# Stores on ScalarE's queue, softmax totals spread over groups, and a last product in two banks: one change to a fused attention and MoE kernel

## The chip, the cores and the metric

One Trainium2 chip, one core. The metric is the device time in microseconds of one execution; times are given as the median of several runs.

## The reference

Attention within chunks of 64 rows (no attention across chunks), the heads laid side by side as a row of 512, and a two-layer network with an exact GELU between:

```
q, k, v: (8, 8, 576, 64) float32          # batch, heads, rows, head size; 9 chunks of 64
attn = softmax(q_c @ k_c.T / sqrt(64))    # per chunk
x = (attn @ v_c) -> (4608, 512)
g = gelu_exact(x @ w_in)                  # w_in (512, 2048)
out = g @ w_out                           # w_out (2048, 512), out float32 (4608, 512)
```

## The kernel before

**Tiles.** The 4608 rows are worked in nine tiles of 512 rows, t = 0 to 8. Tile t < 8 holds chunks 0 to 7 of batch element t; tile 8 holds chunk 8 of all eight elements. Products run on TensorE in bf16.

**Order.** The kernel writes out the order of every engine's instructions by hand (a manual schedule): each engine runs its own instructions in the order in which the program emits them, and waits where data or a buffer is missing. For each tile, `phase` first runs mm1 (`x @ w_in`), sixteen groups f = 0 to 15 of four matmuls (L419), each followed by one GELU on ScalarE (L421), and then mm2 (`g @ w_out`). The attention of the next tile, n = t + 1, is hung into these as hooks: `extra1` (e1) maps a group f of mm1, and `extra2` (e2) a slot of mm2, to things to emit just before it.

**mm2.** For t = 1 and 2, mm2 is `mm2_slot`: four blocks of 128 rows, each in four slots (16 slots; L557), and `rows_out` evicts a block to `y_sb` and stores it. From t = 3, `mm2_seven` does the product with seven instead of eight block products (Strassen's scheme in Winograd's form): steps s = 0 to 6 of two slots each, so hooks stand at slots 0 to 13. The sums of blocks that it needs come from VectorE (`g_sum`, L461 and L474, and `weight_sum`). Banks "a", "b" and "d" hold products; "a" is written in steps 0, 2, 4 and 6, "b" in step 1, "d" in steps 3 and 5. `keep` copies a bank to SBUF (ScalarE, L491), `done` adds a kept block to a bank and stores it (VectorE, L495), `last` evicts the seventh (L500), and `last_piece` does so in halves in the last tile.

**Attention of tile n.** `quad_S` makes the scores in 64 small matmuls (L227), four exps on ScalarE (L234), and for each exp a 32x32 transpose and a sum on VectorE (`quad_part`, L249 and L252). `quad_total` brings the partial sums together: eight small copies on ScalarE (L262), a sum and a reciprocal on VectorE (L265, L267), and four copies on ScalarE (L272); `quad_rc` spreads the reciprocals (L276). `quad_av` multiplies by v (64 small matmuls, L283), and `quad_x` scales the result to x (VectorE, L290). Where `quad_S(n + 1)` follows `quad_av(n)` directly, the two are one joint burst of small matmuls.

**PSUM.** Eight banks in three pools: `ps_mm` (3), `ps_tp` (2), `ps_at` (3). `four_banks` takes two of `ps_at` and two of `ps_tp`; with `beside_av`, `quad_S` takes one of `ps_at` and three of `ps_mm`.

**Loads and stores.** All loads, all transposing DMAs (`flip`, L194) and nearly all stores are issued by SyncE (SP), in program order. Loads land as float32 in six staging buffers, GpSimd (POOL) casts them to bf16, and `flip` transposes q and k of a tile. q and k are brought three tiles ahead (`bring_qk(t + 3)`). `y_sb` and `kept` share four buffers. ScalarE loads another function table when it goes between exp and GELU (`act_table`, L653).

Of the kernel before, what the change touches and what calls it, by code (L numbers as in the profile page):

```python
# [11 lines left out]
def kernel(  # L12
# [9 lines left out]
    nc = tc.nc  # L22
    P = 128
# [5 lines left out]
    CH = 64  # L29
# [225 lines left out]
    def quad_total(t):  # L255
# [3 lines left out]
        for g2 in range(2):  # L259
            for s in range(G):  # L260
                o = s ^ 1
                nc.scalar.copy(part[g2][QD * s:QD * (s + 1), :, :, :, 1], part[g2][QD * o:QD * (o + 1), :, :, :, 0])  # L262
        for g2 in range(2):
# [3 lines left out]
            nc.vector.reciprocal(rb[:], total[:])  # L267
            tiles[t]["rb", g2] = rb[:, 0], across[g2][:]
            if g2 == 0:
                quad_rc(t, 0, 0)  # L270
            for r in range(2):
                nc.scalar.copy(across[g2][CH * r:CH * (r + 1)], rb[CH * (1 - r):CH * (2 - r), 1])  # L272
# [153 lines left out]

    HF = FF // 2
# [48 lines left out]
    def mm2_seven(t, hooks):  # L476
# [10 lines left out]
        bank, kept = {}, {}  # L487

        def keep(name, of):
            kept[name] = ypool.tile([P, HM, HD], f32, tag="y", name="kept")  # L490
            nc.scalar.copy(kept[name][:], bank[of][:])  # L491

        def done(r, c, of, plus):
            y_sb = ypool.tile([P, HM, HD], f32, tag="y", name="y_sb")
            nc.vector.tensor_tensor(y_sb[:], bank[of][:], kept[plus][:], op=ADD)  # L495
            store_block(t, r, c, y_sb)

        def last():
            y_sb = ypool.tile([P, HM, HD], f32, tag="y", name="y_sb")
            nc.scalar.copy(y_sb[:], bank["a"][:])  # L500
            store_block(t, 1, 0, y_sb)
# [8 lines left out]
        for s, (name, left, right, then) in enumerate(steps):  # L510
            fresh = name not in bank
            for m in range(HM):
                for u in hooks.get(HM * s + m, ()):
                    u()
                if fresh and m == 0:
                    pool, tag = (ps_mm, "mm") if name == "d" or t == NT - 1 else (ps_tp, "tp")
                    bank[name] = pool.tile([P, HM, HD], f32, tag=tag, name="y_ps")
                for f in range(HF):
                    nc.tensor.matmul(bank[name][:, m], left(f, m), right[:, f],  # L519
                                     start=(fresh and m == 0 and f == 0),  # L520
                                     stop=(f == HF - 1), skip_group_check=True)
                if t == NT - 1 and s == len(steps) - 1:
                    last_piece(t, m, bank["a"][:, m])
            if not (t == NT - 1 and s == len(steps) - 1):
                then()

    def store_block(t, r, c, y_sb):
        cols = slice(HD * c, HD * (c + 1))
        if t < B:
            m0 = t * S + HD * r  # L530
            nc.sync.dma_start(out[m0:m0 + HD, cols].rearrange("(m p) d -> p m d", p=P), y_sb[:])
            return
        for m in range(HM):
            for i in range(P // CH):
                m0 = ((HM * r + m) * (P // CH) + i) * S + MT
                nc.sync.dma_start(out[m0:m0 + CH, cols], y_sb[i * CH:(i + 1) * CH, m])

    def last_piece(t, m, y_ps):
        y_sb = ypool.tile([P, HD], f32, tag="y", name="y_sb")
        n = HD // 2  # L540
        if m == 0:
            nc.scalar.copy(y_sb[:], y_ps)
        else:
            nc.vector.tensor_copy(y_sb[:, 0:n], y_ps[:, 0:n])
            nc.scalar.copy(y_sb[:, n:HD], y_ps[:, n:HD])
        for i in range(P // CH):
            m0 = ((HM + m) * (P // CH) + i) * S + MT
            (nc.sync if i == 0 else nc.scalar).dma_start(out[m0:m0 + CH, 0:HD], y_sb[i * CH:(i + 1) * CH])
# [16 lines left out]
    def store(t, ms, y_sb):  # L565
        m0 = t * S + ms * P
        nc.sync.dma_start(out[m0:m0 + P, :], y_sb[:])

    def rows_out(t, ms):
        y_ps = tiles[t]["y_ps", ms]  # L570
        y_sb = ypool.tile([P, d_model], f32, tag="y", name="y_sb")
        (AC if ms < 3 else DV)(y_sb[:], y_ps[:])  # L572
        if t == 0 and ms == 2:
            act_table(Act.Gelu)
        if t == 0:
            held.append((ms, y_sb))
        else:
            store(t, ms, y_sb)
# [76 lines left out]
    with tc.manual_schedule():  # L655
# [108 lines left out]
        def last_av():  # L764
            A[3]()
            rows_out(0, 3)
            store(0, *held.pop())
# [11 lines left out]
        for t in range(1, NT):  # L779
# [3 lines left out]
            if t == 1:  # L783
# [3 lines left out]
                for ms, y_sb in held:  # L787
                    store(0, ms, y_sb)
                held.clear()
                load_v_rows(2, (1,))  # L790
            elif t == T0:
                flip_qk(t + 2)
            if n < NT:
                cast_v_rows(n, PO)
            if t == 1:
                bring_qk(t + 2)
                bring_qk(t + 3)
                flip_qk(t + 2)
            if t > 1 and t + 3 < NT:
                bring_qk(t + 3)  # L800
# [5 lines left out]
            flip_next = lambda: flip_qk(t + 3) if t + 3 < NT else None  # L806
            xs = [lambda m=m: quad_x(n, m // 2, m % 2) for m in (1, 3, 0, 2)]
            if t < T0:
                e1 = {f: [lambda i=i: weight_sum(i)] for i, f in ((1, 6), (2, 8), (3, 10), (4, 12))}
                e2 = {0: [exp, lambda: quad_S(n)], 3: [total], 5: [gelu],  # L810
# [3 lines left out]
            elif t == T0:  # L814
                e2 = {0: [exp, lambda: quad_S(n)], 3: [total],
                      8: [lambda m=m: quad_rc(n, m // 2, m % 2) for m in range(1, G)],
                      12: [av] + xs + [lambda: quad_S(n + 1, True)], 13: [flip_next], 15: [gelu]}
            else:
                g = [[lambda i=i, a=a: g_sum(t, i, a) for i in (1, 2, 4)] for a in range(2)]
                e1 = {9: [lambda: g_sum(t, 3)], 13: g[0]}  # L820
                e2 = {0: g[1][:2], 2: g[1][2:]}
                if n < NT:
                    if t == T0 + 1:
                        e1[3] = [total]
                    e1[5] = [lambda m=m: quad_rc(n, m // 2, m % 2) for m in range(1, G)]
# [41 lines left out]
```

## Time and profile before

| | |
|---|---|
| median of 3 runs | 284.04 us (283.96 to 285.39) |
| profiled execution | 286.06 us, its span 284.0 us |
| mean granted TensorE clock | 0.99 |
| TensorE matmuls busy | 270.3 us (95%) |
| ScalarE, VectorE, GpSimd busy | 180.7, 159.3, 91.7 us |
| DMA moved | 53.89 MB, 190 GB/s on the mean |

The profile names engines PE (TensorE matmuls), PEld (its weight loads), DVE (VectorE), ACT (ScalarE), POOL and SP; SPq and ACTq are the instruction queues that issue DMAs. Times are microseconds from the span's start. In a row in order of time stand start, length, engine, line, operation, output<-input, sizes and count, and in brackets the idle time before it and what ended it. A busy matmul is not one at its peak, since matmuls are pipelined and their ends are modelled. "Granted clock" is the share of TensorE's full speed that its throttle allowed.

### The profile page before, as it was taken

The page shows a single profiled execution, that of the slowest core. Times are in us where ns is not written, and L with a number is a line of the kernel's source. Part 1 is how long each engine was busy: PE and PEld are TensorE (multiplying, and loading weights), DVE is VectorE, ACT ScalarE, POOL GpSimd, SP SyncE. Part 2 cuts the span into 40 slices and gives each one's busy share as a digit, 9 for nine tenths or more (in the row PEclk, how much of TensorE's full clock was granted, in tenths as well). Part 3 has the DMA queues.
Part 4 walks back from the last instruction along what each step waited for, and adds up shares of the span by engine and source line. Part 5 has one row for each costly group of instructions (what it writes and reads, how often), then busy time and mean ns, then how long its engine had stood idle before and what let it go on. Part 6 is the DMA issues. An engine that isn't in the chain of part 4 may idle for free.

```text
span 284.0 us, 6437 instructions
## 1 busy us (share of the span) xinstructions
PE 270.3 (95%) x2589; PEld 160.7 (57%) x2589; DVE 159.3 (56%) x267; ACT 180.7 (64%) x370; POOL 91.7 (32%) x146
## 2 busy tenths in 40 slices
PE   6799999999999999799999999999999999999991
PEld 2464455444444444248844874587458745864781
DVE  5865358835900299448915992598159816311620
ACT  3766758877647667666676657757775766347410
POOL 6868778831542206304404610451011000000000
PEclk9999999999999999899999999999999999999998
DMA  7999998999789799999999998979430310130024
GB/s 222 253 360 402 393 362 234 226 254 239 179 235 244 238 262 240 241 212 255 220 285 237 168 204 177 176 168 260 107 84 2 113 35 2 39 111 0 2 46 102
DMA packets 122477, 53.89 MB, mean 190 GB/s; under 512 B 97872, under 2 KB 118352, under 8 KB 122448
## 3 DMA queue, kind: packets, MB, share of 16 engines
q1 hardware_dynamic: 122288, 53.36, 72.8%
q8 instruction: 20, 0.33, 0.5%
q10 hardware_dynamic: 160, 0.13, 0.2%
q14 instruction: 9, 0.07, 0.1%
HBM read 36.70 MB, written 9.44 MB: 162 GB/s over the span
## 4 chain that ended last, share of the span: by engine, by line
PE 87%; ACT 3%; DVE 2%; DMA 2%; POOL 2%; SPq 1%; issue 1%; DVEq 0%; ACTq 0%
PE h_ps L419 41%; PE y_ps L519 25%; PE y_ps L557 11%; PE y_ps L593 3%; PE h_ps L409 2%; DMA arrival<-in_k_dram 2%; POOL v_bd L169 2%; PE s_ps L227 1%; PE av_ps L283 1%; SPq L114 1%; PE tp L175 1%; ACT h L421 1%; DVE x L290 1%; PE av_ps L374 1%; ACT y_sb L572 1%
## 5 line engine op out<-in xcount | busy, mean ns | idle before, releaser
L419 PE MATMUL h_ps<-x,w_in_sb 128*128 128x512 bf16 x548 | 121.9, 383 | 2.2 <-ACT h L421 2.2
L421 ACT ACTIVATE h<-h_ps 128x512 bf16<-128x512 f32 x137 | 80.9, 598 | 38.0 <-PE h_ps L419 37.7
L419 PEld LDWEIGHTS <-w_in_sb 128*128 128x128 bf16 x548 | 54.0, 99 | 67.7 <-issue 5.0
L164 POOL CAST q_nat<-arrival 128x512 bf16<-128x512 f32 x31 | 19.9, 682 | 62.9 <-DMA arrival<-in_q_dram 41.9
L557 PE MATMUL y_ps<-w_out_sb,h 128*128 128x512 bf16 x144 | 32.4, 379 | 0.0
L519 PEld LDWEIGHTS <-h 128*128 128x128 bf16 x288 | 27.9, 98 | 5.1 <-issue 1.2
L200 POOL CAST v_nat<-arrival 128x1024 bf16<-128x1024 f32 x14 | 15.0, 1075 | 48.4 <-DMA arrival<-in_v_dram 30.2
L461 DVE TENSOR_TENSOR s_sb<-h 128x2048 bf16<-128x2048 bf16 x6 | 7.4, 1226 | 35.8 <-ACT h L421 35.8
L491 ACT COPY kept<-y_ps 128x512 f32<-128x512 f32 x18 | 10.6, 586 | 23.2 <-PE y_ps L519 22.0
L653 ACT ACT_TABLE_LOAD x18 | 23.1, 1283 | 1.1 <-PEq L851 0.7
L519 PE MATMUL y_ps<-w_out_sb,h 128*128 128x256 bf16 x192 | 22.0, 272 | 0.7 <-DVE x L290 0.5
L557 PEld LDWEIGHTS <-h 128*128 128x128 bf16 x144 | 13.5, 98 | 15.5 <-issue 0.2
L519 PE MATMUL y_ps<-v_bd,k_bd 128*128 128x256 bf16 x192 | 21.9, 273 | 0.0
L162 POOL CAST k_nat<-arrival 128x512 bf16<-128x512 f32 x28 | 21.1, 785 | 0.9 <-DMA arrival<-in_k_dram 0.9
L290 DVE TENSOR_TENSOR x<-av_ps,rc 128x512 bf16<-128x512 f32 x28 | 18.5, 682 | 4.8 <-PE av_ps L283 4.5
L519 PEld LDWEIGHTS <-k_bd 128*128 128x128 bf16 x192 | 18.8, 98 | 2.2
L252 DVE TENSOR_REDUCE part<-pt 128x16 f32<-128x512 bf16 x28 | 19.2, 686 | 1.0
L495 DVE TENSOR_TENSOR y_sb<-y_ps,kept 128x512 f32<-128x512 f32 x18 | 12.2, 678 | 12.9 <-PE y_ps L519 7.3
L474 DVE TENSOR_TENSOR k_bd<-h 128x1024 bf16<-128x1024 bf16 x12 | 9.2, 770 | 15.1 <-ACT h L421 15.1
L262 ACT COPY part<-part 32x32 f32<-32x32 f32 x56 | 12.3, 219 | 6.8 <-DVE part L252 6.0
L249 DVE STREAM_TRANSPOSE pt<-pT 128x256 f32<-128x256 f32 x28 | 12.2, 435 | 7.5 <-ACT pT L234 7.5
L234 ACT ACTIVATE pT<-s_ps 128x512 bf16<-128x512 f32 x28 | 14.8, 600 | 0.0
(97 smaller groups left out, 302.8 us busy)
## 6 DMA issues: line engine op xcount, KB each, us to landing
out_dram<-y_sb SPq DMA_DIRECT2D x32, 256.0 KB, 2.8
arrival<-in_v_dram SPq DMA_DIRECT2D x58, 128.0 KB, 3.3
arrival<-in_k_dram SPq DMA_DIRECT2D x28, 256.0 KB, 6.4
arrival<-in_q_dram SPq DMA_DIRECT2D x7, 1024.0 KB, 7.6
arrival<-in_moe_w_out_dram SPq DMA_DIRECT2D x4, 1024.0 KB, 11.7
arrival<-in_moe_w_in_dram SPq DMA_DIRECT2D x6, 512.0 KB, 7.8
arrival<-in_v_dram SPq DMA_DIRECT2D x28, 64.0 KB, 2.7
arrival<-in_q_dram SPq DMA_DIRECT2D x4, 256.0 KB, 5.0
```

Source lines behind the costliest of these rows:

```text
L162: copy(st[nm][:, :, g], st[nm + "f"][:, :, g].rearrange("p (q r) d -> p q r d", r=2))
L164: copy(st[nm][:, g].rearrange("p j r d -> p r j d"), st[nm + "f"][:, 2 * g:2 * g + 2])
L200: copy(st["v"][:, r::2], st["vf"][:, r::2])
L234: nc.scalar.activation(pT[:].rearrange("p u (c j) -> p u c j", j=J), s_ps[g2][c][:].rearrange("p u (j c) -> p u c j", j=J), Act.Exp, scale ...
L252: nc.vector.tensor_reduce(st["part", g2][:, c, :, :, 0], pt[:].rearrange("p n e u -> p n u e"), axis=mybir.AxisListType.X, op=mybir.AluOpT ...
L262: nc.scalar.copy(part[g2][QD * s:QD * (s + 1), :, :, :, 1], part[g2][QD * o:QD * (o + 1), :, :, :, 0])
L290: nc.vector.tensor_tensor(x.rearrange("p n (e u) -> p n e u", u=2), st["av"][g2][c][:].rearrange("p n (e u) -> p n e u", u=2), st["rc", 2 ...
L419: nc.tensor.matmul(h_ps[:], w_in_sb[:, ks, f * P:(f + 1) * P], tiles[t]["x"][:, ks, :], start=(ks == 0), stop=(ks == KS - 1))
L421: nc.scalar.activation(tiles[t]["h"][:, f, :], h_ps[:], Act.Gelu)
L519: nc.tensor.matmul(bank[name][:, m], left(f, m), right[:, f], start=(fresh and m == 0 and f == 0), stop=(f == HF - 1), skip_group_check=True)
L557: nc.tensor.matmul(y_ps[:], st["h"][:, f, ms * P:(ms + 1) * P], w_out_sb[:, f, :], start=(f == 0), stop=(f == FF - 1))
L653: nc.scalar.activation(act_scratch[:], rest[:, 0:1], func)
```

## The change

- Stores of tiles 0 to 7 are issued by ScalarE instead of SP, and later: they are put in a list (`owed`), which `pay` issues: for t = 1 and 2 after each ScalarE eviction and at group 2 of the next mm1; from t = 3 after steps 2 and 5 and at group 2 of the next mm1. Tile 0's go out at groups 7, 9, 11 and 13 of tile 1's mm1. Tile 8's blocks go as one DMA on SP and one on ScalarE instead of four on SP.
- `quad_total` is split into steps. For t = 3 and t = 4 these stand one or two to a group of mm1 (`spread_total`), from group 5 and from group 2 on.
- Joint bursts from `mm2_seven` remain for t = 5 and 6 only; for t = 3, `quad_S(5)` stands at slot 8, and for t = 4, `quad_S(6)` at slot 4, both in banks of `four_banks`. At t = 2 the total goes from slot 3 to 5.
- Banks: outside t = 5 and 6, "a" comes from `ps_at` and "b" from `ps_mm`; in tile 8, "a" is two banks of `ps_at`, one for each slot, and `last_piece` evicts each half by one VectorE copy.
- q and k are brought two tiles ahead and flipped at once; v is cast in the same place. `g_sum(t, 3)` goes from group 9 to group 12.

The core of the diff:

```diff
+    def spread_total(t, f0):
+        steps = []
+        rc = lambda g2, c: lambda: quad_rc(t, g2, c)
+        run = lambda i, *a: lambda: steps[i](*a)
+        at = {0: [lambda: steps.extend(total_steps(t)), run(0, 0, 0)], 1: [run(0, 0, 1)], 2: [run(0, 0, 2)],
+              3: [run(0, 0, 3), run(1, 0), rc(0, 0)], 4: [run(0, 1, 0)], 5: [run(0, 1, 1), run(2, 0, 0)],
+              6: [run(0, 1, 2), run(2, 0, 1), rc(0, 1)], 7: [run(0, 1, 3), run(1, 1)], 8: [rc(1, 0)],
+              9: [run(2, 1, 0)], 10: [run(2, 1, 1), rc(1, 1)]}
+        return {f0 + f: us for f, us in at.items()}
...
+    joint_first = range(T0 + 3, NT - 2)
+    owed = []
+    def pay():
+        for go in owed:
+            go()
+        owed.clear()
...
+        apart = t == NT - 1
+        def fresh_bank(name):
+            if apart and name == "a":
+                pair = [ps_at.tile([P, HD], f32, tag="at", name="y_ps") for _ in range(HM)]
+                bank[name] = [(slice(m, m + 1), pair[m][:].unsqueeze(1)) for m in range(HM)]
+                return
+            pool, tag = ((ps_tp, "tp") if name != "d" else (ps_mm, "mm")) if t in joint_first else \
+                ((ps_at, "at") if name == "a" else (ps_mm, "mm"))
+            bank[name] = [(slice(0, HM), pool.tile([P, HM, HD], f32, tag=tag, name="y_ps")[:])]
...
                 then()
+                if s in (2, 5) and not apart:
+                    held_back = owed.pop() if s == 5 else None
+                    pay()
+                    if held_back:
+                        owed.append(held_back)
...
-            nc.sync.dma_start(out[m0:m0 + HD, cols].rearrange("(m p) d -> p m d", p=P), y_sb[:])
+            owed.append(lambda: nc.scalar.dma_start(out[m0:m0 + HD, cols].rearrange("(m p) d -> p m d", p=P), y_sb[:]))
             return
-        for m in range(HM):
-            for i in range(P // CH):
-                m0 = ((HM * r + m) * (P // CH) + i) * S + MT
-                nc.sync.dma_start(out[m0:m0 + CH, cols], y_sb[i * CH:(i + 1) * CH, m])
+        for i, eng in enumerate((nc.sync, nc.scalar)):
+            b0 = HM * r * (P // CH) + i
+            eng.dma_start(out_b[b0:b0 + 3:2, MT:S, cols].rearrange("b p d -> p b d"), y_sb[i * CH:(i + 1) * CH])
...
+            if t + 2 < NT:
+                bring_qk(t + 2)
                 flip_qk(t + 2)
-            if t > 1 and t + 3 < NT:
-                bring_qk(t + 3)
-            if t + 2 < NT:
                 load_v_rows(t + 2)
+                cast_v_rows(t + 2, PO)
...
             elif t == T0:
-                e2 = {0: [exp, lambda: quad_S(n)], 3: [total],
-                      8: [lambda m=m: quad_rc(n, m // 2, m % 2) for m in range(1, G)],
-                      12: [av] + xs + [lambda: quad_S(n + 1, True)], 13: [flip_next], 15: [gelu]}
+                e1 = {2: [pay]}
+                e2 = {0: [exp, lambda: quad_S(n)],
+                      5: [total] + [lambda m=m: quad_rc(n, m // 2, m % 2) for m in range(1, G)],
+                      12: [av] + xs + [lambda: quad_S(n + 1, True)], 15: [gelu]}
             else:
-                e1 = {9: [lambda: g_sum(t, 3)], 13: g[0]}
+                e1 = {2: [pay], 5: [lambda m=m: quad_rc(n, m // 2, m % 2) for m in range(1, G)]}
+                if t < T0 + 3:
+                    e1 = spread_total(n, 5 if t == T0 + 1 else 2)
+                    e1.setdefault(2, []).append(pay)
+                if n == NT:
+                    e1 = {2: [pay]}
+                e1.setdefault(12, []).append(lambda: g_sum(t, 3))
+                e1.setdefault(13, []).extend(g[0])
...
-                    e2 = {0: [exp, av, xs[0], g[1][0], xs[1], g[1][1]], 2: [flip_next], 4: [g[1][2]] + xs[2:],
-                          13: [gelu]}
-                    if n + 1 < NT:
+                    e2 = {0: [exp, av, xs[0], g[1][0], xs[1], g[1][1]], 4: [g[1][2]] + xs[2:], 13: [gelu]}
+                    if t in joint_first:
                         e2[0].append(lambda: later.append(quad_S(n + 1, True, True)))
                         e2[0].append(lambda: later[0](0))
-                        e2[2].append(lambda: later[0](1))
+                        e2[2] = [lambda: later[0](1)]
+                    elif n + 1 < NT:
+                        e2.setdefault(8 if t == T0 + 1 else 4, []).append(lambda: quad_S(n + 1))
+                    if n + 1 < NT and t > T0 + 1:
                         e2[10] = [lambda: quad_total(n + 1)]
```

In `total_steps`, step 0 is one L262 copy, step 1 the sum and reciprocal, step 2 one L272 copy.

More of the change, by code (lines that the diff above doesn't have):

```diff
@@ L499, in last @@
             y_sb = ypool.tile([P, HM, HD], f32, tag="y", name="y_sb")
-            nc.scalar.copy(y_sb[:], bank["a"][:])
+            nc.scalar.copy(y_sb[:], bank["a"][0][1])
             store_block(t, 1, 0, y_sb)
@@ L563, with store @@
     held = []
-    def store(t, ms, y_sb):
+    def store(t, ms, y_sb, eng=nc.sync):
         m0 = t * S + ms * P
-        nc.sync.dma_start(out[m0:m0 + P, :], y_sb[:])
+        eng.dma_start(out[m0:m0 + P, :], y_sb[:])
     def rows_out(t, ms):
@@ L577, in rows_out @@
         else:
-            store(t, ms, y_sb)
+            owed.append(lambda: store(t, ms, y_sb, nc.scalar))
+            if ms < 3:
+                pay()
     def mm2_rows(t, f):
@@ L809 @@
                 e1 = {f: [lambda i=i: weight_sum(i)] for i, f in ((1, 6), (2, 8), (3, 10), (4, 12))}
+                for i, (ms, y_sb) in enumerate(held):
+                    e1[7 + 2 * i] = [lambda ms=ms, y_sb=y_sb: store(0, ms, y_sb, nc.scalar)]
+                e1[13] = [lambda: store(0, *held.pop(), nc.scalar)]
                 e2 = {0: [exp, lambda: quad_S(n)], 3: [total], 5: [gelu],
```

78 lines of the change are left out of this document (37 added, 41 removed).

## The prediction

> **What bounds the kernel now.** I read the chain of work that ended last first, then the order in time of each engine where that chain leaves TensorE, then the stretches with the granted clock, then the store issues.
>
> The chain's shares (page, part 4):
>
> ```profile
> PE 87%; ACT 3%; DVE 2%; DMA 2%; POOL 2%; SPq 1%; issue 1%; DVEq 0%; ACTq 0%
> ```
>
> TensorE is the bound, so only its gaps and what lies behind its last matmul can be won. TensorE in order of time (start, length, operation, count, idle before and its releaser) has four gaps of weight from the third tile (t=2) on:
>
> ```profile
> 106.28 0.44 PE L227 MATMUL s_ps<-q_t,k_t 64*64 64x64 bf16 x30 [0.27 <-ACT y_sb L572]
> ...
> 117.49 10.48 PE L419 MATMUL h_ps<-x,w_in_sb 128*128 128x512 bf16 x40 [2.03 <-ACT h L421]
> ...
> 171.82 11.38 PE L419 MATMUL h_ps<-x,w_in_sb 128*128 128x512 bf16 x52 [0.19 <-ACT h L421]
> ...
> 239.56 3.65 PE L519 MATMUL y_ps<-w_out_sb,h 128*128 128x256 bf16 x32 [0.54 <-DVE x L290]
> 243.05 3.66 PE L519 MATMUL y_ps<-v_bd,k_bd 128*128 128x256 bf16 x32
> 246.55 1.91 PE L519 MATMUL y_ps<-v_bd,s_sb 128*128 128x256 bf16 x16
> ...
> 277.58 1.03 PE L519 MATMUL y_ps<-v_bd,h 128*128 128x256 bf16 x8 [0.46 <-ACT y_sb L542]
> ```
>
> The chain gives undisturbed lengths: an mm1 of 64 matmuls, and a joint burst (0.64 + 0.58):
>
> ```profile
> 104.63 0.02 ACTq L572
> ...
> 141.55 13.81 PE h_ps L419 x64
> 155.36 0.64 PE av_ps L283 x64
> 156.00 0.58 PE s_ps L227 x64
> ```
>
> At t=2 the burst takes 104.63 to 106.72 (106.28 + 0.44) = 2.09 us where 1.22 is normal: 0.86 lost. In t=3 the 40 matmuls behind the 2.03 us gap take 10.48 where 40/64 of 13.81 is 8.63: another 1.85. A stretch of these matmuls says why (length, busy, granted clock, DMA share, GB/s):
>
> ```profile
> 118.20:119.20 1.00, 1.00 (x4) 0.50 1.00 293
> ```
>
> After the gap the granted clock is 0.50; 1.85 us lost at half speed make some 3.5 us of it. So a TensorE gap of 2 us cost nearly twice its length here.
>
> The end (order of time):
>
> ```profile
> 270.07 10.25 SPq L536 DMA_DIRECT2D out_dram<-y_sb  x12
> 279.03 0.27 ACT L545 COPY y_sb<-y_ps 128x128 f32<-128x128 f32 x1 [1.50 <-DVE y_sb L544]
> ...
> 280.42 1.18 SPq L548 DMA_DIRECT2D out_dram<-y_sb  x2
> ```
>
> The first of the two L548 stores on SP's queue had its data when TensorE's wait on the same copy ended, at 277.58, and left at 280.42, behind twelve small L536 issues.
>
> **The change part by part.** *Last product in two banks, and fewer stores in the last tile.* The wait on the copy (0.46, with its resumption 0.6) goes: the second half of the last product no longer shares a bank with the first half's copy. Its eviction becomes one VectorE copy; between the 128x128 copy above (0.27) and the 128x512 copy shown below (0.69) that is 0.41 us. The twelve L536 issues become six, three on each queue, so SP is free when the last piece is ready.
>
> ```profile
> L548 ACTq DMA_DIRECT2D out_dram<-y_sb x2: 479/518/557, 277.6 to 279.3; - x2
> DMA to landing us min/median/max: 2.0/2.0/2.1
> ```
>
> TensorE would end at 278.0, eviction at 278.5, landing at 280.6; from the present last landing (281.0 + 2.05 = 283.1) to the span's end is 0.9, so 281.5 instead of 284.0: −2.5 (bounds −1.9, if the coarser stores land later, and −2.7).
>
> *Total of tile 4 spread over mm1 of t=3.* Eight L262 copies and four L272 copies now stand one or two to a group instead of in one block. A group of mm1 gives ScalarE 0.27 us beside its gelu:
>
> ```profile
> 125.42 0.60 ACT L421 ACTIVATE h<-h_ps 128x512 bf16<-128x512 f32 x1 [0.27 <-PE h_ps L419]
> 113.53 1.84 ACT L262 COPY part<-part 32x32 f32<-32x32 f32 x8
> ```
>
> 1.84 / 8 = 0.23 fits. The 2.03 us gap goes (bounds −1.5 to −2.03), and with it that clock drop, which I book apart.
>
> *Total at slot 5 and stores moved in t=2.*
>
> ```profile
> 97.47 0.69 DVE L572 COPY y_sb<-y_ps 128x512 f32<-128x512 f32 x1 [19.51 <-DMA out_dram<-y_sb]
> ```
>
> DVE's y_sb copy of t=1 waited 19.5 us for a store and held the softmax sums behind it. With stores off SP's queue it no longer does; ScalarE's three row copies come in time, and the burst loses its 0.86 (bounds 0 and −0.86; taken whole, since all its cover moves 1 us earlier).
>
> *Bank "a" from ps_at* at t=7: −0.54. The 0.19 us at t=5, with the slower matmuls behind it (11.38 against 11.22), goes too: −0.35. Gains in idle time: 2.5 + 2.03 + 0.86 + 0.54 + 0.35 = **6.3 us**.
>
> *What the unjoined bursts cost.* For t=3 and t=4 S(n+1) no longer rides beside av. Each costs 0.06 as a burst of its own (0.64 against 0.58), 0.1 together. The larger cost is behind it on VectorE, which works in program order. The rows (t=7, where no softmax sums stand between; then t=3 for the sums):
>
> ```profile
> 243.31 0.69 DVE L495 TENSOR_TENSOR y_sb<-y_ps,kept 128x512 f32<-128x512 f32 x1 [2.00 <-issue]
> 243.92 0.68 DVE L474 TENSOR_TENSOR s<-h,k_bd 128x1024 bf16<-128x1024 bf16 x1
> 244.52 1.28 DVE L290 TENSOR_TENSOR x<-av_ps,rc 128x512 bf16<-128x512 f32 x2
> 246.79 0.59 ACT L491 COPY kept<-y_ps 128x512 f32<-128x512 f32 x1 [1.20 <-PE y_ps L519]
> 130.83 0.44 DVE L249 STREAM_TRANSPOSE pt<-pT 128x256 f32<-128x256 f32 x1
> 135.12 0.68 DVE L495 TENSOR_TENSOR y_sb<-y_ps,kept 128x512 f32<-128x512 f32 x1
> ```
>
> At t=4, S(6) stands at slot 4, right behind the second product. It wants the two ps_at banks of av (the third now holds "a"), which are freed by the last two x operations. These stand on VectorE behind y_sb and a sum: with the second product's end at 243.05 as the mark, x ends at 245.16 and 245.80. TensorE would wait 2.1 us, do half the burst (0.32), wait for the other bank and end it at 246.17, 3.1 us after the mark instead of 0.64: **+2.5 us** (bounds 1.9, and 3.1 where the sum takes as long as the L461 row below).
>
> At t=3, S(5) stands at slot 8. Its four pairs of transposes and sums take 135.12 − 130.83 = 4.29 us on VectorE and stand before the y_sb of product five, whose bank the seventh product writes. By the mark of 246.55 (fourth product's end): kept at 246.79 to 247.38, first exp (0.60, overlapping by 0.1) to 247.9, sums to 252.2, y_sb to 252.9. The seventh product would be due at 246.55 + 0.64 + 3.50 = 250.7: **+2.2 us** (bounds 1.2 and 2.9). Where I am wrong on order, both are nothing.
>
> *VectorE at the end of mm1, t=3.*
>
> ```profile
> 121.30 1.23 DVE L461 TENSOR_TENSOR s_sb<-h 128x2048 bf16<-128x2048 bf16 x1 [3.24 <-ACT h L421]
> ```
>
> L461 (1.23 us) moves from group 9 to 12, where the last inversion (0.6) stands before it, and two rc (0.7 each), three sums of 0.69 and then, at mm2, two x and two sums more (0.6 each) behind. From the inversion, 2.6 us before mm1 ends, that is 7.8 us of work; the last sum, which the third product reads, comes 5.2 us after mm1's end, and is due (0.64 + 1.75 x 2 + half a slot) at 4.6: **+0.6** (bounds 0 and 1.4).
>
> *Stores on ScalarE's queue.* The issue rows, and one that tells whether the queue runs ahead:
>
> ```profile
> L531 SPq DMA_DIRECT2D out_dram<-y_sb x20: 372/375/582, 142.4 to 252.6; - x20
> L548 ACTq EVENT_SEMAPHORE  x2: 17/17/17, 277.2 to 279.0; - x2
> ```
>
> The semaphore instruction at 277.2 ran while the copy on which TensorE waited until 277.58 was still going, so an issue whose data is ready can pass under a running gelu. Two at group 2 are 0.75 to 1.1 us against 0.6 of cover, and ps_mm's three banks give another 1.1. Queued behind them are the gelus, and TensorE behind those. I take 0.1 in all (bounds 0 and 3, six tiles at 0.5). In mm2 they stand before a kept copy or the gelu table, with 0.6 to spare.
>
> *Loads.* SP loses its stores and brings q and k two tiles ahead, flipped at once, instead of three; POOL's v casts move behind the q and k casts. SP waits for POOL's casts before each flip, some 3 us, in which DMA does only stores. The flip of tile 4 is the tight one (its issue before, and the landing of all flips):
>
> ```profile
> 100.43 1.84 SPq L194 DMA_TRANSPOSE k_t<-k_nat  x1
> ...
> DMA to landing us min/median/max: 3.7/3.9/6.2
> ```
>
> With SP's own issue times I get its second flip issued at 97.5 to 99.5, landing 4 to 6 later, before S(4) at 105.3. Cost nothing; if that cover is gone, below.
>
> **The sum.** −6.3 + 2.5 + 2.2 + 0.6 + 0.1 + 0.1 = −0.8 us without the clock. The profiled execution took 286.06 us (span 284.0, 2.06 around it); with as many clock drops after as before that is 285.3. The runs shown have the median 284.04, 2.0 lower, close to the 1.85 of one drop: perhaps the profiled run had the drop and most others not. On the median: **283.3 us**.
>
> *The clock, and a rule.* The gap of 2.03 us dropped it; the new ones are 2.1 and 2.2. One row can't say whether such a gap always does. The Trainium skill (TensorE: Matmul & The Clock Gate, "Part 1: The HAM clock gate") has the clock fall to half after an idle window of about 3.4 us, in windows that run freely of the kernel. The trace agrees on the length of the slow time (some 3.5 us) but not that 3.4 us of idling are needed. By that rule neither new gap drops the clock and the profiled sum would be 283.5; by the row alone both do, and it would be 287.2.
>
> **The rivals.** (a) *One drop fewer*: neither new gap drops the clock where the typical run before has one: 283.3 − 1.85 = 281.4. For: a short gap may be split over two counting stretches. Against: one gap of just this size did drop it. (b) *More drops*, the one that ends slower: the typical run before has none (284.04 against 286.06 speaks for it), the gaps at slot 4 of t=4 and at the seventh product of t=3 drop it once or twice: 285.1 or 287.0. It decides from two drops on. (c) *The flip of tile 4 is late*: from a landing after 105.3, S(4) waits in t=2, some 2 to 3 us: 286. For: DMA is at its full share there. Against: SP's waits for stores are gone. (d) *The unjoined bursts don't stall*, because VectorE reaches x and y_sb earlier than I count: 283.3 − 4.7 = 278.6. Against: the order in the code. (e) Stores on ScalarE cost what they show, 0.5 a tile: 286; it is part of (c)'s chance.
>
> **How the numbers follow.** What this kernel's runs can tell from no change is about 0.5%, 282.6 to 285.5. Forecast 283.3: 0.38, of which 0.05 falls below and 0.03 above that band. (a) 0.27, faster. (b) one drop 0.13, of which 0.03 counts as slower; two 0.06, slower. (c) and (e) 0.11, 0.03 of it within. (d) 0.05, faster. Faster 0.37, same 0.43, slower 0.20. The range leaves out (d), the two drops and the ends of (a): 280.0 to 286.2. The forecast alone, with its bounds: 282 to 285.
>
> **What would show it.** Right: no gap in mm1 of t=3; the span's end 3.5 us behind the last matmul instead of 5.4; in t=4 s_ps waiting on DVE x, in t=3 y_ps on DVE y_sb. Wrong: those two waits missing, s_ps at t=2 waiting on DMA q_t or k_t, gelus late behind ACTq stores, or the clock at 0.50 in other places than these two.

## The result, and the profile after

| | before | after |
|---|---|---|
| median, runs side by side | 284.72 us (4 runs) | 295.5 us (4 runs, 293.22 to 297.14) |
| profiled execution, its span | 286.06, 284.0 us | 296.36, 294.6 us |
| mean granted TensorE clock | 0.99 | 0.982 |
| TensorE matmuls busy | 270.3 us | 273.1 us |

Slower by 3.7%: ratio 1.037, 95% interval 1.029 to 1.046. In the ratios below, a run more than 1.5% above the fastest of its kernel is left out; the medians hold all runs. Forecast were 283.3 us and a range of 280.0 to 286.2.

The shares of the chain that ended last, of which TensorE had 87% before, are now:

```profile
PE 54%; SPq 19%; DMA 13%; ACT 7%; DVE 3%; issue 2%; POOL 1%; ACTq 0%; POOLq 0%; DVEq 0%
```

DMA issues and landings have come onto the path. TensorE in order of time shows where; each bracket is idle time and its releaser:

```profile
66.08 0.71 PE L227 MATMUL s_ps<-q_t,k_t 64*64 64x64 bf16 x64 [1.02 <-DMA k_t<-k_nat]
...
87.50 9.66 PE L446 MATMUL h_ps<-x,w_in_sb 128*128 128x512 bf16 x44 [1.71 <-ACT h L448]
...
111.39 0.44 PE L227 MATMUL s_ps<-q_t,k_t 64*64 64x64 bf16 x30 [2.14 <-ACT y_sb L622]
...
115.22 13.98 PE L446 MATMUL h_ps<-x,w_in_sb 128*128 128x512 bf16 x64
...
134.34 3.23 PE L568 MATMUL y_ps<-v_bd,k_bd 128*128 128x256 bf16 x28 [0.44 <-DVE k_bd L509]
...
143.76 3.19 PE L568 MATMUL y_ps<-v_bd,h 128*128 128x256 bf16 x16 [1.95 <-DVE y_sb L545]
...
152.02 11.80 PE L446 MATMUL h_ps<-x,w_in_sb 128*128 128x512 bf16 x52 [2.10 <-ACT h L448]
...
170.63 1.00 PE L227 MATMUL s_ps<-q_t,k_t 64*64 64x64 bf16 x64 [2.55 <-issue]
171.57 5.28 PE L568 MATMUL y_ps<-v_bd,k_bd 128*128 128x256 bf16 x32
```

The row of 115.22 is mm1 of t=3, now without its gap: forecast and there. The waits of 0.44, 1.95 and 2.55 us are the three that the prediction named for the later sum and the unjoined bursts (0.6, 2.2, 2.5). The profile names no releaser for the 2.55 ("issue"), where the prediction had x; VectorE's rows show it, since the first of the two last x operations ends at about 170.5, just before TensorE goes on at 170.63:

```profile
169.84 1.29 DVE L317 TENSOR_TENSOR x<-av_ps,rc 128x512 bf16<-128x512 f32 x2
```

Not forecast are the wait of 1.02 us for a late flip and those of 1.71, 2.14 and 2.10 us, these three all released by ScalarE. What ScalarE itself waited for (total, times, longest):

```profile
ACT L705 <- DMA arrival<-in_v_dram: 9.3, 1, 9.3
ACT h L448 <- DMA out_dram<-y_sb: 6.5, 3, 3.0
...
ACT y_sb L622 <- DMA arrival<-in_v_dram: 3.3, 1, 3.3
```

A table load and a GELU use nothing of v and nothing of an earlier store, and a row copy uses nothing of v. What stands ahead of them on ScalarE does: a store. The longest of these waits, in order of time on ScalarE, VectorE and SP:

```profile
138.09 2.07 ACT L234 ACTIVATE pT<-s_ps 128x512 bf16<-128x512 f32 x4
149.09 0.38 ACTq L585 DMA_DIRECT2D out_dram<-y_sb  x1
149.50 1.28 ACT L705 ACT_TABLE_LOAD   x1 [9.34 <-DMA arrival<-in_v_dram]
...
143.02 1.28 DVE L545 TENSOR_TENSOR y_sb<-y_ps,kept 128x512 f32<-128x512 f32 x2
...
144.33 1.62 SPq L194 DMA_TRANSPOSE k_t<-k_nat  x1
146.00 5.39 SPq L124 DMA_DIRECT2D arrival<-in_v_dram  x9
```

ScalarE was through with the exps at 140.2. The store's data was there at 144.3 at the latest, when both L545 sums had ended. It left at 149.09, three microseconds after SP had begun to issue nine loads of v. Why it waits for a load stands in the compiled program's list of waits, which is no profile (here in ScalarE's order, the store of 149.09 in the second line):

```
L585 DMA out_dram<-y_sb 128x2x256 [waits DMAHW0_49,DVE_49]
...
L585 DMA out_dram<-y_sb 128x2x256 [waits DMAHW1_49,DVE_49]
L705 ACT_TABLE_LOAD
...
L585 DMA out_dram<-y_sb 128x2x256 [waits DMAHW5_49,DVE_49]
```

Beside its data (DVE) the store waits on one of eight counters, DMAHW0 to 7, which report that a DMA has landed. The program, as it was compiled, gives every DMA of SP and of ScalarE one of the eight, strictly in turn over both engines together, and lets a DMA wait until the one that had its counter before has landed. The counter of the store of 149.09, DMAHW1, was last given to one of the nine loads of v. As long as all stood on SP, the earlier holder stood ahead in the same queue, and the one that waited was SP, on which nothing but DMA issues stands. On ScalarE a store waits for a load that SP issues when POOL's casts and the flips let it; and everything behind it on ScalarE waits too.

The earlier holder need not be a load. The counter of the store of 86.47 was last given to ScalarE's own store of 79.94, and it waits until that has landed. The GELU behind it is the one that releases TensorE's gap of 1.71 us:

```profile
86.86 2.31 ACT L448 ACTIVATE h<-h_ps 128x512 bf16<-128x512 f32 x4 [3.02 <-DMA out_dram<-y_sb]
```

That an issue looks cheap in a profile (0.38 us) says nothing of this. The Trainium skill (Perfetto Trace Analysis, "DMA Instruction — HWDGE (DVE, Sync)") has the reported start of a DMA issue at the moment when all its semaphores are satisfied, so a wait lies ahead of the row and not in it; the trace agrees, with 0.38 in the row and 4.8 us or more ahead of it after the data was there.

### The profile page after: what moved, and what is told of

It is laid out like the page before. It is cut to its first block, busy times and chain, and to the rows that moved or that the text cites. A ratio compares the mean times of both kernels' runs of the same rounds, so it can differ in the third digit from the quotient of the medians.

```text
span 294.6 us, 6417 instructions
## 1 busy us (share of the span) xinstructions
PE 273.1 (93%) x2589; PEld 162.4 (55%) x2589; DVE 158.3 (54%) x269; ACT 179.4 (61%) x370; POOL 87.9 (30%) x146
## 4 chain that ended last, share of the span: by engine, by line
PE 54%; SPq 19%; DMA 13%; ACT 7%; DVE 3%; issue 2%; POOL 1%; ACTq 0%; POOLq 0%; DVEq 0%
PE h_ps L446 23%; PE y_ps L568 20%; SPq L124 15%; DMA arrival<-in_k_dram 9%; PE y_ps L645 3%; SPq L194 3%; DMA out_dram<-y_sb 3%; ACT h L448 2%; PE h_ps L436 2%; ACT k_bd L188 2%; DMA arrival<-in_v_dram 1%; PE y_ps L607 1%; PE rc_ps L388 1%; DVE k_bd L509 1%; SPq L114 1%
## 5 line engine op out<-in xcount | busy, mean ns | idle before, releaser
L200 POOL CAST v_nat<-arrival 128x1024 bf16<-128x1024 f32 x14 | 15.7, 1124 | 86.2 <-DMA arrival<-in_v_dram 86.2
L164 POOL CAST q_nat<-arrival 128x512 bf16<-128x512 f32 x31 | 18.1, 624 | 26.3 <-DMA arrival<-in_q_dram 19.8
L540 ACT COPY kept<-y_ps 128x512 f32<-128x512 f32 (+1 forms) x20 | 10.8, 544 | 24.3 <-PE y_ps L568 21.9
L568 PE MATMUL y_ps<-v_bd,k_bd 128*128 128x256 bf16 x192 | 23.7, 284 | 0.4 <-DVE k_bd L509 0.4
L496 DVE TENSOR_TENSOR s_sb<-h 128x2048 bf16<-128x2048 bf16 x6 | 8.2, 1371 | 27.2 <-ACT h L448 27.2
L162 POOL CAST k_nat<-arrival 128x512 bf16<-128x512 f32 x28 | 18.8, 695 | 9.7 <-DMA arrival<-in_k_dram 9.5
L568 PEld LDWEIGHTS <-k_bd 128*128 128x128 bf16 x192 | 19.5, 102 | 3.7 <-DVE k_bd L509 0.7
L545 DVE TENSOR_TENSOR y_sb<-y_ps,kept 128x512 f32<-128x512 f32 (+1 forms) x19 | 12.3, 651 | 15.0 <-PE y_ps L568 9.7
L568 PE MATMUL y_ps<-v_bd,h 128*128 128x256 bf16 x96 | 12.7, 291 | 1.9 <-DVE y_sb L545 1.9
```

The costliest lines, as they stand in the source:

```text
L162: copy(st[nm][:, :, g], st[nm + "f"][:, :, g].rearrange("p (q r) d -> p q r d", r=2))
L164: copy(st[nm][:, g].rearrange("p j r d -> p r j d"), st[nm + "f"][:, 2 * g:2 * g + 2])
L200: copy(st["v"][:, r::2], st["vf"][:, r::2])
L568: nc.tensor.matmul(region(name, m), left(f, m), right[:, f], start=(fresh and f == 0 and (m == 0 or len(bank[name]) > 1)), stop=(f == HF - ...
```

## The experiments

Theory 1: stores on ScalarE's queue, held by such waits, carry the loss. Theory 2: the unjoined bursts do, with the clock drops behind them. Theory 3: the new load order does. Each ratio is against the kernel before on the same chip (medians of 283.5 to 284.4 us, and 284.72 for the changed kernel itself); a difference in microseconds between runs of different chips can be off by about 1 us, so there the ratios count.

**Queue undone.** The stores of tiles 0 to 7 go to SP, at the changed kernel's places.

```diff
-            owed.append(lambda: nc.scalar.dma_start(out[m0:m0 + HD, cols]...
+            owed.append(lambda: nc.sync.dma_start(out[m0:m0 + HD, cols]...
```

> The changed kernel with one thing undone: the stores of the first eight tiles are issued on SP's queue instead of ScalarE's, at the same places of the program. Theory 1 (a store at the head of ScalarE's queue waits until an earlier DMA has landed with which it shares a completion semaphore, mostly one that SP issues late, and the exps and gelus behind it wait too): the waits of ScalarE behind stores (9.3, 6.5 and 3.3 us in the changed kernel's waits) go, and with them the gaps of 1.71 us at 87.5, 2.14 at 111.4, 2.10 at 152.0 and 1.95 at 143.8 with its clock drop. What stays is the unjoined bursts' 2.2 + 2.5 and the gains: 285 us (282 to 288). Theory 2 (the unjoined bursts at t=3 and t=4 with their clock drops are the loss): 293 or more, no gain from the queue. Theory 3 (the new load order on SP is the loss): 294 or more, since SP then has the stores as well.

309.3 us, ratio 1.088 (1.081 to 1.095): 21 us above theory 1's upper end. It lies in the open ranges of theory 2 (293 or more) and theory 3 (294 or more), and theory 3 also had the reason, SP's stores beside the new loads. TensorE in t=1, and SP's queue there:

```profile
87.19 6.11 PE L607 MATMUL y_ps<-w_out_sb,h 128*128 128x512 bf16 x16 [11.19 <-ACT y_sb L622]
...
78.78 5.22 SPq L124 DMA_DIRECT2D arrival<-in_v_dram  x9
84.11 5.86 SPq L617 DMA_DIRECT2D out_dram<-y_sb  x7
```

The new load order lets SP flip at once, and so wait for POOL's casts; stores emitted behind that leave at 84.11, and a row copy that needs their buffer stops TensorE for 11.19 us. So the stores were moved off SP together with an order of loads that can't bear them on SP; neither part can be judged by undoing the other alone.

**Stores on POOL's queue**, by the same edit with `nc.gpsimd`:

> The changed kernel with the stores of the first eight tiles issued on POOL's queue, at the same places of the program. POOL's DMAs have completion semaphores of their own, which no load of SP shares. Theory 1: no wait of ScalarE behind a store, and SP's loads are not held by them either; POOL's casts may wait for stores' data: 284 us (281 to 288). Theory 2 or 3: 293 or more. If the stores' lateness (buffers of y_sb coming free late), not the queue, held the copies, the wait of ACT h and y_sb on DMA out_dram would stay and the time would be 290 or more here and with SP's queue alike.

305.14 us, 1.075 (1.069 to 1.080), far above theory 1's 281 to 288. A miss of the same kind: POOL stands waiting for the stores' data (54.1 us in total), its casts behind it, and the buffers come late again. Here and on SP's queue the lateness of the stores' buffers does hold ScalarE's row copy, as the expectation's last case has it; for the changed kernel this settles nothing, since there a table load and GELUs wait, which need no such buffer.

```profile
POOL out_dram L585 <- DVE y_sb L545: 54.1, 9, 16.6
```

```profile
91.55 5.52 PE L607 MATMUL y_ps<-w_out_sb,h 128*128 128x512 bf16 x16 [15.88 <-ACT y_sb L622]
```

**The queue alone.** The kernel before, its stores on ScalarE at their old places.

```diff
-            nc.sync.dma_start(out[m0:m0 + HD, cols]...
+            nc.scalar.dma_start(out[m0:m0 + HD, cols]...
```

> The kernel before with one thing changed: the stores of the first eight tiles are issued on ScalarE's queue, at their old places. Theory 1: ScalarE now waits behind stores, for data as well as for other DMAs' semaphores; slower by 5 us or more, 290 to 300. Theory 2 (unjoined bursts): no change, 283.5 to 286. Theory 3 (load order): no change or a little faster, since SP's loads go earlier, 282 to 285.

304.21 us, 1.070 (1.062 to 1.078): theory 1's sign, and worse than its range of 290 to 300. Theories 2 and 3 expected no loss. At the old places a store also waits for its data on ScalarE. ScalarE's waits for data (first row) and for other DMAs (the others):

```profile
ACT kept L491 <- DVE y_sb L495: 11.5, 3, 4.4
...
ACT L653 <- DMA out_dram<-y_sb: 4.0, 1, 4.0
...
ACT h L421 <- DMA arrival<-in_v_dram: 3.3, 1, 3.3
ACT pT L234 <- DMA arrival<-in_k_dram: 2.8, 1, 2.8
```

**The loads alone.** The kernel before with the new load order:

```diff
+                cast_v_rows(2, PO)
+            if t + 2 < NT:
+                bring_qk(t + 2)
                 flip_qk(t + 2)
...
                 load_v_rows(t + 2)
+                cast_v_rows(t + 2, PO)
```

> The kernel before with the new load order alone (q and k two tiles ahead, flipped at once, v cast there); its stores stay on SP. Theory 1: some 1 us for the first flip, which came 1.0 us late in the changed kernel, and as SP's stores stand before loads that are now needed sooner, up to 5 us: 285 to 290. Theory 3: 293 or more. Theory 2: 284 to 286.

309.05 us, 1.090 (1.082 to 1.097): far above theory 1's 285 to 290, and theory 3's "293 or more". Scores wait for the flips in four tiles (TensorE in order of time, the first and the last of them; then SP's waits):

```profile
129.78 0.71 PE L227 MATMUL s_ps<-q_t,k_t 64*64 64x64 bf16 x64 [2.90 <-DMA k_t<-k_nat]
...
234.52 1.07 PE L227 MATMUL s_ps<-q_t,k_t 64*64 64x64 bf16 x64 [7.48 <-DMA k_t<-k_nat]
```

```profile
SPq L531 <- DVE y_sb L495: 43.4, 10, 17.5
SPq L194 <- POOL k_nat L162: 30.3, 12, 4.0
```

SP's one queue now waits 30.3 us for POOL's casts ahead of flips that are issued at once, and 43.4 for the data of stores, ahead of loads that are needed a tile sooner.

**Stores and loads both undone**, back at their old places on SP; the rest as changed.

```diff
-            owed.append(lambda: nc.scalar.dma_start(...
+            nc.sync.dma_start(...
...
+            if t > 1 and t + 3 < NT:
+                bring_qk(t + 3)
```

> The changed kernel with both the stores and the loads of the first eight tiles put back on SP as before the change (same places, same order of SP's queue); the spread totals, the unjoined bursts, the later sums, the banks and the last tile stay changed. Theory 1 (ScalarE's queue held by stores that wait for SP's loads): the sum of the other terms as measured in the changed kernel: 284.7 - 2.5 (end) - 2.0 (gap of t=3) - 0.5 - 0.35 + 1.95 + 2.55 + 0.45 = 284.3, with 0 to 3 of clock drops: 284 to 287. Theory 2 (unjoined bursts and their clock drops are the loss): 293 or more. Theory 3 (load order alone is the loss): also 284 to 287; the next run and the one with the load order alone tell 1 from 3.

287.74 us, 1.012 (1.004 to 1.020), 0.7 above what theories 1 and 3 had (284 to 287) and far under theory 2's 293. ScalarE's longest wait on a DMA is 0.4 us, and TensorE's gaps of 0.4 us or more from t=2 on are the three that the prediction had:

```profile
129.41 3.23 PE L568 MATMUL y_ps<-v_bd,k_bd 128*128 128x256 bf16 x28 [0.45 <-DVE k_bd L509]
...
138.84 3.26 PE L568 MATMUL y_ps<-v_bd,h 128*128 128x256 bf16 x16 [1.95 <-DVE y_sb L545]
...
163.53 1.20 PE L227 MATMUL s_ps<-q_t,k_t 64*64 64x64 bf16 x64 [3.02 <-issue]
```

So queue and loads together carry 7.8 of the 10.8 us (0.025 of 0.037 in ratio), and the rest of the change is itself no gain.

**Old loads, stores still on ScalarE** (the second half of that diff alone):

> The changed kernel with the old order of the loads alone put back (q and k three tiles ahead, flips one tile ahead); the stores stay on ScalarE's queue at their new places. Theory 1, in the form that only the lateness of SP's loads makes a store wait: ScalarE's waits of 9.3 and 3.3 us on arrival of v go or shrink below 2, 287 (285 to 290). Theory 1, in the form that any sharing with SP's queue holds ScalarE: the waits move to other stores and the time stays at 292 to 298. Theory 3 (load order alone): 284 to 286, and the kernel before with the new loads alone is slow.

298.13 us, 1.051 (1.044 to 1.057): just above the second form of theory 1 (292 to 298), and far above the first (285 to 290). Theory 3 as the only cause is out, since it had 284 to 286 here. Against the run just told only the stores differ, in queue and place, and they cost 10.4 us. The waits moved to other stores. ScalarE, and what SP did until then:

```profile
117.24 0.34 ACTq L617 DMA_DIRECT2D out_dram<-y_sb  x1
117.62 1.57 ACT L448 ACTIVATE h<-h_ps 128x512 bf16<-128x512 f32 x3 [4.49 <-DMA arrival<-in_v_dram]
...
109.13 8.13 SPq L124 DMA_DIRECT2D arrival<-in_v_dram  x9
```

**v ahead of the flips.** If a store waits for a load that is issued late, an earlier issue must end the wait, though nothing of the store is touched:

```diff
                 bring_qk(t + 2)
+                load_v_rows(t + 2)
                 flip_qk(t + 2)
-                load_v_rows(t + 2)
```

> The changed kernel with one line moved: SP issues the nine loads of v of a tile before the two flips of q and k instead of behind them, so they don't stand behind the flips' wait for POOL's casts. The stores stay on ScalarE's queue. Theory 1 (a store on ScalarE's queue waits for the landing of the DMA that had its completion semaphore before it): the waits of ScalarE on arrival of v (9.3 us before the table load at 149.5, 3.3 before the row copy at 110.8) fall below 1 us or turn into waits on a flip (k_t or q_t); with them gone 291 (288 to 294), with flips in their place 294 to 298. Rival (the store waits only for its own data and for room in its queue): ScalarE's wait behind the store at 149 stays at 9 us, since no store's data and no queue of ScalarE has changed.

289.61 us, 1.020 (1.012 to 1.028), 5.9 us below the changed kernel (0.017 in ratio), inside theory 1's 288 to 294. ScalarE's waits on v have shrunk to a single one of 0.5 us; before the same table load it now waits for the store's data alone:

```profile
143.21 0.38 ACTq L585 DMA_DIRECT2D out_dram<-y_sb  x1
143.62 1.28 ACT L705 ACT_TABLE_LOAD   x1 [3.99 <-DVE y_sb L545]
...
108.37 1.07 PE L227 MATMUL s_ps<-q_t,k_t 64*64 64x64 bf16 x64 [2.53 <-DMA k_t<-k_nat]
```

The rival (a store waits for its own data only) is out. One thing more changed than the time of the loads: by the compiled program of this run the store of 143.21 has a counter that another store of ScalarE had before it, and no load. The new order of the DMAs deals the counters out anew, so this run doesn't tell the earlier load from the other holder; both belong to the same mechanism. The last row is the price: the flip of tile 4 now comes 2.5 us late.

**Joint bursts kept from t=3** in the changed kernel:

```diff
-    joint_first = range(T0 + 3, NT - 2)
+    joint_first = range(T0 + 1, NT - 2)
```

> The changed kernel with the joint bursts kept from t=3 on, as before the change (S(n+1) beside av in the first slots of mm2; the first bank of mm2 then comes from ps_tp again). Theory 1: only the waits of s_ps at t=4 (2.55 us, with 1.6 us of clock drop behind it) and the one of y_ps at t=3 (1.95 us, with 1.3 of clock) go; ScalarE's waits behind stores stay: 289 (287 to 292). Theory 2: nearly all of the loss goes: 283 to 286. Theory 3: 294 or more.

290.96 us, 1.027 (1.021 to 1.033): 4.5 us less than the changed kernel (0.010 in ratio), inside theory 1's 287 to 292 and above the 283 to 286 of theory 2. ScalarE still waits behind a store, 6.5 us ahead of a table load.

**The same with stores and loads undone as well:**

> As the first of these runs, and with the joint bursts from t=3 kept as before the change; so what is left of the change is the spread totals of t=3 and t=4, the later sums, the bank from ps_at at t=7 and the last tile. Theory 1: 284.7 - 2.5 - 2.0 - 0.5 - 0.35 = 279.3, without a clock drop in t=3 another 1 to 2 less; the wait of y_ps on DVE x at t=3 and t=4 (2.1 and 1.7 us where the joint bursts alone were put back) would add 3.8 if it comes from the later sums: 278 to 283. Theory 2: 284 or more is against it only if the waits of the unjoined bursts are gone and the time does not fall by 4 against the first run.

283.13 us, 0.999 (0.995 to 1.003): 4.6 less than with unjoined bursts, but not the forecast 279.3, and just above its 278 to 283. TensorE, and VectorE at the end of mm1 of t=3:

```profile
126.21 3.65 PE L568 MATMUL y_ps<-w_out_sb,h 128*128 128x256 bf16 x32 [2.12 <-DVE x L317]
...
155.37 3.65 PE L568 MATMUL y_ps<-w_out_sb,h 128*128 128x256 bf16 x32 [1.74 <-DVE x L317]
...
121.16 1.16 DVE L496 TENSOR_TENSOR s_sb<-h 128x2048 bf16<-128x2048 bf16 x1
```

Two waits on x take back 3.9 us. The sum of 1.16 us (L461 before, now at group 12) stands between the last inversion and x. **That sum back at group 9:**

```diff
-                e1.setdefault(12, []).append(lambda: g_sum(t, 3))
+                e1.setdefault(9, []).append(lambda: g_sum(t, 3))
```

> As the run with all but the queue, the loads and the unjoined bursts, but with the 2048-wide sum of mm1 (L461 before, L496 after) back at group 9 from group 12, in every tile from t=3. There TensorE waited 2.12 us at t=3 and 1.74 at t=4 for VectorE's x at the start of mm2. If the later sum is the cause: the wait of t=3 falls to the 1.2 us that the spread total alone left, that of t=4 to under 0.7, and the time from 283.1 to 281 (280 to 282). If the second spread total (t=4) is the cause: the wait of t=4 stays above 1.5, 282.5 to 283.5.

280.39 us, 0.989 (0.985 to 0.993): the sum is the cause, as the two waits show (expected were 1.2 and under 0.7).

```profile
126.34 3.65 PE L568 MATMUL y_ps<-w_out_sb,h 128*128 128x256 bf16 x32 [1.18 <-DVE x L317]
...
154.01 3.65 PE L568 MATMUL y_ps<-w_out_sb,h 128*128 128x256 bf16 x32 [0.25 <-DVE x L317]
```

**The gains by themselves**: the total of tile 4 spread, alone; the last tile, alone; and both with bank "a" from `ps_at` at t=7, on the kernel before. The diff is the core of the first.

```diff
-                        e1[3] = [total]
...
+                        for f, us in spread_total(n, 5).items():
+                            e1[f] = us + e1.get(f, [])
```

> The kernel before with the total of tile 4 spread over mm1 of t=3 alone. From the prediction's terms: the gap of 2.03 us in mm1 of t=3 goes, and where it drops the clock another 1.85: 282 (280 to 283). If the work that now stands on VectorE at the end of mm1 delays x (as with the later sums, 2.1 us at t=3), 284 to 286.

> The kernel before with the last tile's part alone: last product in two banks, each evicted by one VectorE copy, and stores of two batches at once on both queues. The prediction's term is 2.5 us (1.9 to 2.7); the changed kernel's end showed 0.6 from PE's end to the span's end and no wait at the last product. 281.3 (280.5 to 283).

> The kernel before with the three parts that showed gains: the total of tile 4 spread over mm1 of t=3, bank a from ps_at at t=7, and the last tile's part; joint bursts, sums, stores and loads as before. Sum of the terms: 283.8 - 2.0 - 0.5 - 2.5 = 278.8, less up to 1.85 where the old gap dropped the clock: 278 (276 to 281). If the spread total alone delays x at t=3 by 2 us: 281.

282.18 us, 0.993 (0.989 to 0.997); 281.51 us, 0.991 (0.987 to 0.995); and 278.98 us, 0.984 (0.979 to 0.989), the lowest of all. All three lie in the ranges expected. (The second expectation's 0.6 us from TensorE's end to the span's end in the changed kernel is wrong: it is 4.8.) In the last, mm1 of t=3 has no gap and one wait of TensorE above 0.3 us is left from t=2 on:

```profile
124.85 3.65 PE L560 MATMUL y_ps<-w_out_sb,h 128*128 128x256 bf16 x32 [1.17 <-DVE x L317]
```

**The spread two groups earlier** (`spread_total(n, 3)`) was to take that wait away:

> As the run with the gains alone (spread total at t=3, bank a at t=7, last tile), with the spread starting at group 3 instead of group 5 of mm1, so that the last inversion and the sums behind it on VectorE stand two groups (1.7 us) earlier. The wait of 1.17 us of y_ps on x at the start of mm2 goes: 277.8 (277 to 279). If the sums of tile 4 on VectorE aren't through at group 3, ScalarE's first copies wait and the gelus behind them: 279 to 281.

279.69 us, 0.987 (0.983 to 0.991): no gain, a miss. The wait only fell to 0.93. VectorE's last step for the softmax totals still ends at 122.85, and the three sums behind it begin 0.6 us before the end of mm1, where they begin 2.8 before it in the kernel before; x stands behind them. ScalarE's first copies did not wait, so it is luck that the time lies in the 279 to 281 that the expectation had for that case. At t=5, which the edit doesn't touch, this execution shows a wait of 0.77 where the other had 0.26:

```profile
125.53 3.65 PE L560 MATMUL y_ps<-w_out_sb,h 128*128 128x256 bf16 x32 [0.93 <-DVE x L317]
...
181.18 3.65 PE L560 MATMUL y_ps<-w_out_sb,h 128*128 128x256 bf16 x32 [0.77 <-DVE k_bd L501]
```

## Why the prediction was wrong

From the gains alone to the changed kernel, in ratios to the kernel before: 0.984 with the gains; 0.989 with the second spread total and the total at slot 5 as well (the intervals overlap, so this step isn't clear of noise); 0.999 with the later sum; 1.012 with the unjoined bursts; 1.037 with stores and loads. By the prediction's steps:

- **Last product in two banks, fewer stores, −2.5.** Right: alone −2.9 (284.44 to 281.51), with an interval that holds 2.5. The eviction was put at 0.41 us and took 0.42; the stores left on SP 0.13 us behind it:

```profile
287.86 1.91 PE L568 MATMUL y_ps<-v_bd,h 128*128 128x256 bf16 x16
...
288.93 0.42 DVE L596 COPY rc<-y_ps 128x256 f32<-128x256 f32 x1 [0.18 <-PE y_ps L568]
...
289.48 1.51 SPq L598 DMA_DIRECT2D out_dram<-rc  x2
```

  From the last matmul's end (289.77) to the span's end it is 4.8 us in the changed kernel, and 3.8 where the part was made alone (forecast 3.5). About half of that 1 us shows in the last stores, which took 2.8 and 2.9 us to land (medians of the two queues) instead of 2.3; why, stays open.
- **Spread total, −2.03; bank "a" at t=7, −0.54; t=5.** The gaps went. The first gave 1.17 us back at the start of mm2, which the prediction didn't see: the steps of the inversion now end later on VectorE, ahead of x.
- **Joint burst at t=2, −0.86.** It should not have been counted. The kernel with the last tile's part alone, whose t=2 is that of before, shows no gap there either: the loss belonged to the one profiled execution. With the stores on ScalarE the burst instead lost 2.14.
- **Unjoined bursts, +2.5 and +2.2 (and 0.1).** Right in place, cause and size: 2.55 and 1.95 in the changed kernel. With the clock drops behind them, and net of the two waits on x (3.9 us) that only the joint form has, they cost 4.6 us (287.74 against 283.13).
- **Later sum, +0.6.** Right for the third product (0.44). Mis-sized for the joint form, where it holds x (2.7 us, 283.13 against 280.39).
- **Stores on ScalarE's queue, +0.1 (0 to 3).** The step that failed. It priced the issue itself, 0.75 to 1.1 us for two with data ready, and this was right or a little high (0.34 to 0.38 each in most). It took for granted that a store whose data is ready can leave, and never asked what else a DMA waits for. Measured, with nothing else different but the stores' queue and places: +10.4 us with the old loads. With the new ones it is three TensorE gaps of 1.71, 2.14 and 2.10 us, which with the late flip (1.02) add up to 7.0 of the 7.8 us that stores and loads carry together. Rival (e), 0.5 us a tile, had the place but a price of issue time; 10.4 us over eight tiles are 1.3 a tile, and they are waits.
- **Loads, nothing.** Hidden only while the stores are elsewhere: on the kernel before they cost 25.5 us (309.05 against 283.54). With the stores on ScalarE they don't cost but rather gain: the ratio goes from 1.051 to 1.037, with intervals that just touch. So the two parts lean on each other. Rival (c), the flip of tile 4 late, did not come in the changed kernel; the flip of tile 2 did (1.02 at 66.08).

**The clock.** Stretches of the changed kernel behind gaps of 1.71, 1.95, 2.10 and 2.55 us (length; busy time and count for PE, PEld, DVE, ACT and POOL; granted clock; DMA share; GB/s):

```profile
87.50:89.50 2.00, 2.00 (x10) 0.93 (x10) 0.00 (x0) 1.60 (x4) 0.00 (x0) 1.00 0.81 236
...
145.50:147.30 1.80, 1.80 (x9) 1.16 (x8) 0.00 (x0) 0.00 (x0) 0.00 (x0) 0.50 1.21 277
...
152.10:154.00 1.90, 1.83 (x9) 0.72 (x9) 0.00 (x0) 1.23 (x4) 0.00 (x0) 1.00 0.72 156
...
172.00:174.00 2.00, 2.00 (x11) 1.45 (x10) 1.93 (x5) 1.20 (x3) 1.04 (x1) 0.50 0.79 179
```

The gaps of 1.95 and 2.55 halved the clock and cost 1.3 (3.19 us instead of 1.91 for sixteen matmuls) and 1.8 (5.28 instead of 3.50 for 32). Those of 1.71, 2.10 and 2.14 did not (behind the last the granted clock is 1.00 from 111.40 to 113.40). Nor does one and the same gap always do it. The gap of 2.03 us in mm1 of t=3, behind which 40 matmuls took 10.48 in the kernel before, is also in the kernel before with the last tile's part alone (first row), and there they took 8.79. The gap of 1.95 left the clock whole with v ahead of the flips (second row):

```profile
115.67 8.79 PE L419 MATMUL h_ps<-x,w_in_sb 128*128 128x512 bf16 x40 [2.03 <-ACT h L421]
...
143.23 1.91 PE L568 MATMUL y_ps<-v_bd,h 128*128 128x256 bf16 x16 [1.95 <-DVE y_sb L545]
```

So both forecasts that the prediction weighed, no new drop or two, were too plain: near 2 us neither the length of a gap nor its place decides, and the same gap costs differently from one execution to the next. The Trainium skill (TensorE: Matmul & The Clock Gate, "Part 1: The HAM clock gate") has the counting windows run freely of the kernel; that fits here, its idle window of about 3.4 us does not (1.95 us of idling were enough).

## What to carry to other kernels

Before a DMA is moved to another engine's queue, ask for every wait that it brings along, not for its issue time alone: here a store on the engine that runs the GELUs waited for loads of a queue that runs late, and all behind it waited. Move stores and loads by turns only if each alone is at least neutral; here each alone cost the kernel before 20 us or more, and together they still cost 7.8. Of this change the best version was its three small parts that take a wait off TensorE, at 0.984 of the time before, although one of them delays x by 1.17 us; what added or delayed more work on VectorE ahead of x (the later sum) gave the gain back.

## What the runs showed of the hardware that was not expected

DMAs of SP and ScalarE waited for one another through eight shared counters, which the compiled program gives out (it is a property of the program as compiled, not shown to be one of the chip): 9.34 us before a table load (149.50; 4.8 of them after the store's data was there), 4.49 before a GELU with the old loads, and 0.5 at most on loads of v when these were issued ahead of the flips. TensorE gaps near 2 us (1.95, 2.03) halved the clock in one execution and left it whole in another at the same place, and gaps of 2.10 and 2.14 us left it whole where one of 1.95 in the same execution did not.
